# Store and read order at the start of an attention kernel: the first chunk's reads ahead of the second chunk's stores, stores in halves, rows six groups ahead

## The chip, the cores and the metric

One core of one Trainium2 chip runs the whole program. The metric is device time in microseconds (us), the median of several runs. KB are 1024 bytes, as the profile counts them.

## The reference

The reference is an attention layer that mixes its heads before and after the softmax, followed by two dense blocks. The inputs of the attention are 4 batches of 12 heads, 448 rows, 64 columns each.

```python
scores = scale * np.matmul(q, k.transpose(0, 1, 3, 2))
scores = np.einsum('bhij,hg->bgij', scores, w_pre)
scores = scores - np.max(scores, axis=-1, keepdims=True)
attn = np.exp(scores)
attn = attn / (np.sum(attn, axis=-1, keepdims=True) + 1e-09)
attn = np.einsum('bhij,hg->bgij', attn, w_post)
x = np.matmul(attn, v)          # then to 1792 tokens x 768
h = (x @ w1) * (x @ w2) @ w3
x = h @ w_out
h = x @ w_in
out = np.maximum(0.01 * h, h) @ w_out2
```

## The kernel before

The attention comes first, the two dense blocks ("MoE" in the code) after it; this change is all in the first 100 us or so. A batch of 448 rows is cut into four *chunks* of 120, 120, 120 and 88 rows. A chunk is cut into blocks of ten rows, and two blocks make a *group*: a chunk of 120 has six groups, one of 88 has five, the four batches have 92.

One chunk passes through these steps, which the trace shows by tile name and line:

- `qk` (tile `pq`, L203): scores of one pair of heads for all the chunk's rows; ScalarE (and VectorE for the first two chunks) copies them to a tile `s`.
- `flush` (`sdr<-s`, L236): SyncE's queue (SP) stores the scores of two pairs to DRAM. A whole chunk of 120 rows is three stores.
- `relayout` (`sr<-sdr`, L250): SP reads one group's rows back with heads on the partitions, two DMAs a group. It waits for the stores that hold those rows.
- `premix` (`pm`, L261): TensorE mixes the heads of a group.
- softmax on VectorE, ScalarE and GpSimd.
- `postmix` (`po`, L304): TensorE mixes heads again and transposes.
- `av` (`px`, L324): TensorE multiplies with the values `vs`, which `v_prep` (L174) loads once for a batch.

The order is written out by hand. A prologue computes the scores of the first two chunks (`order[0]`, `order[1]`) and starts their stores and reads. Then a loop takes two groups at a time (a *step*): first the stores that have become ready, `qk` of the chunk two ahead, the reads of groups `AHEAD` further on, softmax, `av` of an earlier chunk, `postmix` of the last step's groups, further loads (`side`), and `premix` of the next step's groups. All DMAs of the attention are issued by SP, one after the other; a DMA that waits holds up all behind it. The first `av` stands in the step after the groups 4 and 5 are done, behind `premix` of groups 8 and 9, and `vs` of the first batch is issued in step 2.

The first chunk's stores go in halves of 60 rows already (`HALVES`); groups 0 to 2 need the first half alone.

Of the kernel before, what the change touches and what calls it, by code (L numbers as in the profile page):

```python
# [22 lines left out]
def attention_moe_kernel(ctx: ExitStack, tc, qt, kt, vt, w_pre, w_post, w1, w2, w3t, w_out, w_in2, w_out2, out):  # L23
# [8 lines left out]
    B, _, NPAIR, S = kt.shape  # L32
# [7 lines left out]
    JP = 112  # L40
    NJ = S // JP
    IB = 10
    AHEAD, QAHEAD, HALVES = 4, 2, 2
    HP = 2
    CH = qt.shape[-1]
    scale = 1.0 / float(D) ** 0.5
# [20 lines left out]
    ps = ctx.enter_context(tc.tile_pool(name="ps", bufs=2, space=PSUM))  # L67
    def bank(shape, name):
        return ps.tile(shape, F32, tag="bank", name=name, bufs=8)
# [34 lines left out]
    ends, reads, marks = {}, [], []  # L104

    def attention():
        with ExitStack() as es:
# [47 lines left out]
            kls, qls, stores = {}, {}, []  # L155
# [32 lines left out]
            def qk(b, c, p):  # L188

                m = cols[c]  # L190
                g, r = divmod(p, HP)
                first = (b, c) == order[0]
                if first and p == 0:
                    st[b, c] = late.tile([CH, H, S], F32, tag="ap", name="s", bufs=2)
                elif not first and r == 0:
                    st[b, c] = big.tile([CH, 2 * HP, S], F32, tag="s", name="s", bufs=5)
                t = st[b, c][:, 2 * g * HP:2 * (g + 1) * HP] if first else st[b, c]
                first_two = order.index((b, c)) < QAHEAD
                pq = [bank([CH, S], "pq") for _ in range(2)]
                for j, (x, y) in enumerate(((0, 0), (0, 1), (1, 0))):  # L200
                    for e in range(2):
                        rows = slice(e * D, (e + 1) * D)
                        nc.tensor.matmul(  # L203
                            pq[e][:m], qst[b, c][rows, p, x, :m], kst[b, p][rows, y, :], start=(j == 0), stop=(j == 2)
                        )
                def out():
                    for e in range(2):
                        if e and first_two:
                            nc.vector.tensor_copy(t[:m, 2 * r + e, :], pq[e][:m])
                        else:  # L210
                            nc.scalar.activation(out=t[:m, 2 * r + e, :], in_=pq[e][:m], func=ACTF.Copy)  # L211
                    if r == HP - 1:
                        heads = slice(2 * g * HP, 2 * (g + 1) * HP)
                        if first:
                            n = m // HALVES
                            for i in range(HALVES):
                                stores.append((sdr[b, c][i * n:(i + 1) * n, heads, :], t[i * n:(i + 1) * n]))
                        else:
                            stores.append((sdr[b, c][:, heads, :], t[:m]))

                evs.append(out)
                if first_two:
                    evict()

            evs = []

            def evict():
                while evs:
# [2 lines left out]
            def flush(n=None):  # L231

                while stores and n != 0:
                    n = n and n - 1
                    dst, t = stores.pop(0)
                    nc.sync.dma_start(out=dst, in_=t)  # L236

            def turn(n):

                t = bank([P, P], "turn")  # L240
                for _ in range(n):
                    nc.tensor.matmul(t, ones, ones, start=True, stop=True)  # L242

            def relayout(k):

                sr = srt[k] = wk.tile([P, 2, S], F32, tag="sr", name="sr", bufs=6)
                for s, n in enumerate(groups[k]):
                    b, c, o, nb = blocks[n]
                    src = sdr[b, c][o:o + nb].rearrange("(g i) h j -> (i h) g j", g=2)
                    last = nc.sync.dma_start(out=sr[s * Q:s * Q + nb // 2 * H], in_=src)  # L250
                reads.append(last)
                ends["sync"] = last

            def premix(k):

                sr = srt.pop(k)
                for s, n in enumerate(groups[k]):
                    pms[n] = bank([P, S], "pm")
                    rows = slice(s * Q, s * Q + blocks[n][3] // 2 * H)
                    for g in range(2):  # L260
                        nc.tensor.matmul(  # L261
                            pms[n][g * Q:(g + 1) * Q], kpre[rows], sr[rows, g, :], start=True, stop=True
                        )
# [77 lines left out]
            order = [(b, c) for b in range(B) for c in range(NC)]  # L341
            blocks = [(b, c, o, nb) for b, c in order for o, nb in chunks[c][2]]
            groups, where = [], []
# [5 lines left out]
            NG = len(groups)  # L349
# [15 lines left out]
            for p in range(NPAIR):  # L365
                qk(*order[0], p)
                if p < NPAIR - 1:
                    turn(2 if p < 3 else 1)
                    flush()
                if p == 0:  # L370
                    for low in [k_split(0, 4, nc.gpsimd), k_split(0, 5, nc.gpsimd)]:
                        low()
            q_split(*order[1])()
            constants()
            flush(1)
            for k in range(2):
                relayout(k)
            flush()
            for k in range(2, AHEAD):
                relayout(k)  # L380
            for p in range(NPAIR):
                qk(*order[1], p)
                flush()
            turn(2)
            q_split(*order[2])()

# [2 lines left out]
            def at(step, *job):  # L389

                jobs.setdefault(max(step, 0), []).append(job)
# [14 lines left out]
            for i in range(QAHEAD + 1, len(order)):  # L406
                s0 = firsts[i - QAHEAD] // 2
                at(max(s0 - 2, 2), "qs", *order[i])
                at(s0 - 5, "ql", *order[i])
            for b in range(B):  # L410
                g0 = firsts[b * NC]
                at(g0 // 2 + 2, "v", b)
# [4 lines left out]
                        if p % 2 == 0:  # L417
                            at((g0 + p) // 2 - (4 if b > 1 else 3), "kl", b, p // 2)

            def pairs(k):  # L420

                b, c, t, nt = where[k]
                ci = order.index((b, c))
                if ci + QAHEAD >= len(order):
                    return []
                ps = [4, 5] if nt < NPAIR and t == 4 else [t]
                return [(*order[ci + QAHEAD], p) for p in ps]

            premix(0)
            premix(1)  # L430
            todo = []
            for k in range(0, NG + 2, 2):
                flush()
                while later:
                    stores.append(later.pop(0))
                now = [g for g in (k, k + 1) if g < NG]
                done = [g for g in (k - 2, k - 1) if g >= 0]
                fresh = [n for g in now for n in groups[g]]
                old = [n for g in done for n in groups[g]]
                for g in now:  # L440
                    for x in pairs(g):
                        qk(*x)
                for g in now:
                    if g + AHEAD < NG:
                        relayout(g + AHEAD)
                if fresh:
                    tops(fresh)
                    sm = softmax(fresh)
                evict()
                if now:  # L450
                    for _ in range(min(4 if len(todo) > NPAIR else 2, len(todo))):
                        av(*todo.pop(0))
                    weigh(fresh, sm)
                while lows:
                    lows.pop(0)()
                for i, n in enumerate(old):
                    on_act = i == 1 or i == 3 and k >= firsts[-1 - QAHEAD + 1]
                    postmix(n, nc.scalar.copy if on_act else nc.vector.tensor_copy)
                side(k // 2)
                if k == 4:  # L460
                    while lows:
                        lows.pop(0)()
                for g in done:
                    b, c, t, nt = where[g]
                    if t == nt - 1 and (b, c) != order[-1]:
                        todo += [(b, c, p) for p in range(NPAIR)]
                for g in (k + 2, k + 3):
                    if g < NG:
                        premix(g)
                marks.append(dict(ends))  # L470
# [10 lines left out]
    def moe():  # L481
        with ExitStack() as es:
# [11 lines left out]
            NT = T // P  # L494
            NH = DM // 2
            FQ = 4
            XREADS, XMARKS = (-5, -3), (-5, -5, -4, -4, -4, -4, -3, -3, -3, -2, -2, -2)
            PARTS = ((0, 512), (512, T - 512))

            def behind(mark):  # L500
# [77 lines left out]
            plan = []  # L578
# [91 lines left out]
            for s in range(B // 2):  # L670
                xx = xs[s]
                h = hg.tile([P, KF, 2, T], F32R, tag="hg", name="h")
                for m in range(KF):
# [6 lines left out]
                    for n in range(2):  # L680
                        pb = mm(wb, xx, KM, n)
                        w = PARTS[n][1]
                        at = wk.tile([P, w], F32, tag="at", name="at")
# [10 lines left out]
                for f in range(0, KF2, FQ):  # L694
                    g = hg.tile([P, FQ, 2, T], F32R, tag="hg", name="g")
                    for m in range(FQ):
                        wt = next_w()
                        for n in range(2):
                            pg = mm(wt, x2, KM, n)
                            w = PARTS[n][1]  # L700
                            at = wk.tile([P, w], F32, tag="at", name="gt")
# [25 lines left out]

    attention()
    moe()


# [49 lines left out]
```

## Time and profile before

| | us |
|---|---|
| median of 3 runs (1295.18 to 1295.81) | 1295.79 |
| the profiled execution | 1296.19 |
| its span, first to last instruction | 1294.4 |
| TensorE (PE) busy in the span | 1279.2 |

The profiled execution is 0.40 us above the median, and its time is 1.8 us longer than its span. A stretch of the span is read by its windows (busy time of each engine, granted TensorE clock as a share of full speed, share of time in which the 16 DMA engines are busy, bytes moved), and a wait by what ended it.

### The profile page before, as it was taken

The page shows a single profiled execution, that of the slowest core. Times are in us where ns is not written, and L with a number is a line of the kernel's source. Part 1 is how long each engine was busy: PE and PEld are TensorE (multiplying, and loading weights), DVE is VectorE, ACT ScalarE, POOL GpSimd, SP SyncE. Part 2 cuts the span into 40 slices and gives each one's busy share as a digit, 9 for nine tenths or more (in the row PEclk, how much of TensorE's full clock was granted, in tenths as well). Part 3 has the DMA queues.
Part 4 walks back from the last instruction along what each step waited for, and adds up shares of the span by engine and source line. Part 5 has one row for each costly group of instructions (what it writes and reads, how often), then busy time and mean ns, then how long its engine had stood idle before and what let it go on. Part 6 is the DMA issues. An engine that isn't in the chain of part 4 may idle for free.

```text
span 1294.4 us, 22410 instructions
## 1 busy us (share of the span) xinstructions
PE 1279.2 (99%) x8926; PEld 1127.2 (87%) x8926; DVE 867.4 (67%) x1441; ACT 601.9 (46%) x1169; POOL 117.3 (9%) x192
## 2 busy tenths in 40 slices
PE   7899999999999999999999999999999999999998
PEld 5577777777778989999899999999898889999998
DVE  4565675675668999833485969695673459687662
ACT  5665666676655554522254524352332236434240
POOL 1232232232321000000000000000000000000000
PEclk8899999999999999999999999999999999999999
DMA  7998988988885654733334423363321424342302
GB/s 221 302 319 228 268 261 268 285 266 226 256 261 168 185 163 142 228 115 88 123 105 140 126 95 122 98 218 127 119 82 49 133 77 149 98 147 74 123 1 86
DMA packets 132072, 211.57 MB, mean 163 GB/s; under 512 B 19393, under 2 KB 115649, under 8 KB 131521
## 3 DMA queue, kind: packets, MB, share of 16 engines
q1 hardware_dynamic: 131969, 210.15, 52.6%
q8 instruction: 71, 1.16, 0.4%
q14 instruction: 32, 0.26, 0.1%
HBM read 157.43 MB, written 52.69 MB: 162 GB/s over the span
## 4 chain that ended last, share of the span: by engine, by line
PE 96%; DMA 3%; DVE 1%; ACT 0%; issue 0%; SPq 0%; DVEq 0%
PE pm L619 45%; PE po L716 18%; PE po L304 11%; PE pm L261 6%; PE px L324 6%; PE pw L530 5%; PE pq L203 4%; DMA sr<-sdr 2%; DMA vs<-in_v_dram 1%; PE turn L242 1%; DMA sdr<-s 0%; DVE wc L96 0%; DVE x L75 0%; ACT s L211 0%; DVE ap L311 0%
## 5 line engine op out<-in xcount | busy, mean ns | idle before, releaser
L619 PE MATMUL pm<-x,ws 128*128 128x512 f32 (+1 forms) x2304 | 467.0, 364 | 0.2 <-ACT ws L72 0.2
L619 PEld LDWEIGHTS pm<-x,ws 128*128 128x128 f32 x2304 | 417.6, 188 | 48.0 <-ACT ws L72 0.3
L716 PE MATMUL po<-ws,g 128*128 128x384 f32 x1344 | 234.3, 334 | 0.0
L716 PEld LDWEIGHTS po<-ws,g 128*128 128x128 f32 x1344 | 233.1, 188 | 0.0
L304 PE MATMUL po<-kr,e 128*112 128x120 f32 (+1 forms) x1440 | 159.7, 270 | 0.0
L277 ACT ACTIVATE e<-pm,mx 128x448 f32<-128x448 f32 x180 | 111.8, 632 | 100.0 <-DVE mx L270 99.6
L304 PEld LDWEIGHTS po<-kr,e 128*112 128x112 f32 x1440 | 151.2, 178 | 7.5 <-issue 6.3
L75 DVE TENSOR_TENSOR ws<-wc,ws 128x768 fp32r<-128x768 f32 (+1 forms) x112 | 102.5, 918 | 69.6 <-ACT ws L72 69.0
L72 ACT ACTIVATE ws<-wc 128x768 fp32r<-128x768 f32 (+1 forms) x112 | 90.8, 813 | 113.6 <-PE po L716 73.9
L91 ACT ACTIVATE wc<-wr 128x768 f32<-128x768 f32 (+1 forms) x120 | 104.9, 877 | 78.0 <-DVE ws L75 57.5
L290 POOL TENSOR_SCALAR kr<-kpost,rc 128x120 f32<-128x120 f32 x180 | 113.1, 644 | 276.2 <-DVE rc L287 144.4
L311 DVE COPY ap<-po 112x480 f32<-112x480 f32 (+1 forms) x129 | 83.8, 653 | 55.8 <-PE po L304 55.4
L270 DVE TENSOR_REDUCE mx<-pm 128x1 f32<-128x448 f32 x180 | 101.2, 618 | 25.0 <-PE pm L261 24.6
L619 PE MATMUL pm<-h,ws 128*128 128x512 f32 (+1 forms) x576 | 116.3, 363 | 0.0
L619 PEld LDWEIGHTS pm<-h,ws 128*128 128x128 f32 x576 | 104.3, 188 | 11.7
L99 DVE SCALAR_TENSOR_TENSOR wc<-wr,wc 128x768 uint32<-128x768 uint32 (+1 forms) x120 | 110.3, 920 | 1.6
L96 DVE SCALAR_TENSOR_TENSOR wc<-wr,wc 128x768 uint32<-128x768 uint32 (+1 forms) x120 | 110.0, 919 | 0.9
L261 PE MATMUL pm<-sr,kpre 60*64 60x448 f32 (+1 forms) x720 | 86.0, 567 | 7.0 <-DMA sr<-sdr 6.9
L92 DVE TENSOR_SCALAR wc<-wc 128x768 f32<-128x768 f32 (+1 forms) x120 | 64.8, 540 | 37.9 <-ACT wc L91 37.4
L324 PEld LDWEIGHTS px<-ap,vs 112*64 112x64 f32 x1536 | 73.9, 137 | 17.1 <-ACT e L277 8.2
L723 DVE TENSOR_TENSOR acc<-po,acc 128x384 f32<-128x384 f32 x84 | 46.2, 557 | 62.1 <-PE po L716 61.3
L211 ACT ACTIVATE s<-pq 120x448 f32<-120x448 f32 (+1 forms) x180 | 84.1, 560 | 4.7 <-PE pq L203 4.0
(54 smaller groups left out, 952.8 us busy)
## 6 DMA issues: line engine op xcount, KB each, us to landing
sr<-sdr SPq DMA_DIRECT2D x176, 210.0 KB
wr<-in_moe_w_out_dram SPq DMA_DIRECT2D x40, 768.0 KB
sdr<-s SPq DMA_DIRECT2D x33, 840.0 KB
wr<-in_moe_w_dram SPq DMA_DIRECT2D x32, 768.0 KB
wr<-in_moe_w_in_dram SPq DMA_DIRECT2D x32, 768.0 KB
wr<-in_moe_w_dram SPq DMA_DIRECT2D x16, 512.0 KB
sdr<-s SPq DMA_DIRECT2D x12, 616.0 KB
wf<-w SPq DMA_DIRECT2D x12, 512.0 KB
```

Source lines behind the costliest of these rows:

```text
L75: nc.vector.tensor_tensor(out=dst, in0=src, in1=hi.bitcast(F32), op=ALU.subtract)
L91: nc.scalar.activation(out=cf, in_=hi.bitcast(F32), func=ACTF.Abs)
L96: nc.vector.scalar_tensor_tensor(out=c, in0=hi, scalar=0xC0000000, in1=c, op0=ALU.bitwise_and, op1=ALU.bitwise_or)
L99: nc.vector.scalar_tensor_tensor(out=c, in0=lo, scalar=29, in1=c, op0=ALU.logical_shift_right, op1=ALU.bitwise_or)
L261: nc.tensor.matmul(pms[n][g * Q:(g + 1) * Q], kpre[rows], sr[rows, g, :], start=True, stop=True)
L270: nc.vector.tensor_reduce(out=mxs[n], in_=pms[n], axis=AX.X, op=ALU.max, negate=True)
L277: ends["act"] = nc.scalar.activation(out=ets[n], in_=pms.pop(n), func=ACTF.Exp, bias=mxs.pop(n), scale=1.0, accum_out=sm[:, i:i + 1])
L290: ends["pool"] = nc.gpsimd.tensor_scalar(out=kr[:, i], in0=kpost, scalar1=rc[:, i:i + 1], scalar2=None, op0=ALU.mult)
L304: nc.tensor.matmul(po[:, jc].rearrange("p h (g i) -> p h g i", g=2), e[:, jc * JP:(jc + 1) * JP], kr, start=True, stop=True,)
L324: nc.tensor.matmul(px[e * D:(e + 1) * D, r, :ni], vst[b][:, jc, 2 * p + e, :], ap[:, jc, 2 * p + e, :ni], start=(jc == 0), stop=(jc == NJ ...
L619: nc.tensor.matmul(dst, wt[:, a, kk, :], x[:, kk, c, c0:c0 + w], start=(kk == 0 and j == 0), stop=(kk == kn - 1 and j == 2),)
L716: nc.tensor.matmul(po, g[:, m, a, t * P:(t + 1) * P], wts[m][:, c, 0, cs], start=(m == 0 and j == 0), stop=(m == FQ - 1 and j == 2),)
```

## The change

Nothing is computed otherwise; the same DMAs and matmuls run in another order, and six stores of half the size take the place of three for the second chunk.

- First chunk: of its six half stores, those of the first half of the rows (and one of the second half) go first, then the reads of groups 0 and 1, then the other two halves, then the reads of groups 2 to 5.
- The load of the fourth chunk's q comes next, before the second chunk's stores.
- Second chunk: its stores go in halves too: three first halves and one second half, the reads of groups 6 and 7, and the other two second halves.
- `AHEAD` is 6: groups are read up to six (or eight) ahead, as soon as their chunk's last store was issued one step ago (two, for the further ones).
- The scores of the third chunk are spread over four steps, where they took three.
- The marks behind which the dense block reads its input (`XREADS`) move with the reads.

```diff
-    AHEAD, QAHEAD, HALVES = 4, 2, 2
+    AHEAD, QAHEAD, HALVES = 6, 2, 2
...
+                    if p == NPAIR - 1:
+                        stored[b, c] = step[0]
                     if r == HP - 1:
-                        if first:
+                        if first_two:
                             n = m // HALVES
...
             for p in range(NPAIR):
                 qk(*order[0], p)
                 if p < NPAIR - 1:
                     turn(2 if p < 3 else 1)
+                if p < 3:
                     flush()
...
-            flush(1)
+            late_halves = [stores.pop(i) for i in (1, 2)]
+            flush()
             for k in range(2):
                 relayout(k)
+            stores += late_halves
             flush()
             for k in range(2, AHEAD):
                 relayout(k)
+            q_load(*order[3])
             for p in range(NPAIR):
                 qk(*order[1], p)
-                flush()
+            late_halves = [stores.pop(i) for i in (3, 4)]
+            first_late = stores.pop(1)
+            stores.append(first_late)
+            flush()
...
-                at(s0 - 5, "ql", *order[i])
+                if i > QAHEAD + 1:
+                    at(max(s0 - 5, 2), "ql", *order[i])
...
+            plan = {}
+            for g, (b, c, t, nt) in enumerate(where):
+                ci = order.index((b, c)) + QAHEAD
+                if ci < len(order):
+                    ps = [4, 5] if nt < NPAIR and t == 4 else [t]
+                    for p in ps:
+                        i = (0, 0, 1, 2, 2, 3)[p] if ci == QAHEAD else g // 2
+                        plan.setdefault(i, []).append((*order[ci], p))
...
             premix(0)
             premix(1)
+            for k in range(AHEAD, AHEAD + 2):
+                relayout(k)
+            stores += late_halves
...
-                for g in now:
-                    if g + AHEAD < NG:
-                        relayout(g + AHEAD)
+                for g in range(len(reads), min(k + AHEAD + 2, NG)):
+                    ago = step[0] - stored.get(where[g][:2], step[0])
+                    if ago < (1 if g < k + AHEAD else 2):
+                        break
+                    relayout(g)
...
-            XREADS, XMARKS = (-5, -3), (-5, ...)
+            XREADS, XMARKS = (-3, -1), (-5, ...)
```

SP's queue from the first chunk's stores to the load of `vs`, before. `sdr_0`, `sdr_1`, `sdr_2` are the first three chunks' scores in DRAM; two DMAs `sr<-sdr` make a group.

```order
L236 DMA sdr_0_57<-s 60x1792
L250 DMA sr<-sdr_0_57 60x2x448 x4
L236 DMA sdr_1_58<-s 120x1792 x3
L250 DMA sr<-sdr_0_57 60x2x448 x4
L178 DMA ql<-in_q_dram 128x720
L236 DMA sdr_2_59<-s 120x1792
L250 DMA sr<-sdr_1_58 60x2x448 x4
L178 DMA ql<-in_q_dram 128x720
L236 DMA sdr_2_59<-s 120x1792
L250 DMA sr<-sdr_1_58 60x2x448 x4
L174 DMA vs<-in_v_dram 112x3072
```

Ahead of the first of these rows stand five of the first chunk's half stores and the reads of groups 0 and 1. The same stretch of SP's queue in the changed kernel, from the first chunk's stores on:

```order
L238 DMA sdr_0_57<-s 60x1792 x4
L252 DMA sr<-sdr_0_57 60x2x448 x4
L238 DMA sdr_0_57<-s 60x1792 x2
L252 DMA sr<-sdr_0_57 60x2x448 x8
L178 DMA ql<-in_q_dram 128x720
L238 DMA sdr_1_58<-s 60x1792 x4
L252 DMA sr<-sdr_1_58 60x2x448 x4
L238 DMA sdr_1_58<-s 60x1792 x2
L238 DMA sdr_2_59<-s 120x1792
L252 DMA sr<-sdr_1_58 60x2x448 x8
L178 DMA ql<-in_q_dram 128x720
L174 DMA vs<-in_v_dram 112x3072
```

The reads of groups 4 and 5 moved ahead of the second chunk's stores, and `vs` now stands behind the reads of groups 10 and 11 instead of behind the third chunk's second store.

TensorE's queue from the third pair of premixes (groups 4 and 5) to the first `px`, before:

```order
L261 MATMUL pm<-sr,kpre 64x448 x8
L203 MATMUL pq<-ks,qs 120x448 x12
L304 MATMUL po<-kr,e 112x120 x16
L261 MATMUL pm<-sr,kpre 64x448 x8
L203 MATMUL pq<-ks,qs 88x448 x12
L304 MATMUL po<-kr,e 112x120 x16
L261 MATMUL pm<-sr,kpre 64x448 x8
L203 MATMUL pq<-ks,qs 88x448 x12
L324 MATMUL px<-ap,vs 64x120 x16
```

And in the changed kernel:

```order
L263 MATMUL pm<-sr,kpre 64x448 x8
L203 MATMUL pq<-ks,qs 120x448 x12
L306 MATMUL po<-kr,e 112x120 x16
L263 MATMUL pm<-sr,kpre 64x448 x8
L203 MATMUL pq<-ks,qs 120x448 x6
L203 MATMUL pq<-ks,qs 88x448 x12
L306 MATMUL po<-kr,e 112x120 x16
L263 MATMUL pm<-sr,kpre 64x448 x8
L203 MATMUL pq<-ks,qs 88x448 x12
L326 MATMUL px<-ap,vs 64x120 x16
```

One pair of the third chunk (six matmuls) moved a step later; the first `px` has the same work ahead of it in sum.

## Rows read from the trace of the kernel before

**Rows 1.** The page: span, and busy time of each engine.

```profile
span 1294.4 us, 22410 instructions
PE 1279.2 (99%) x8926; PEld 1127.2 (87%) x8926; DVE 867.4 (67%) x1441; ACT 601.9 (46%) x1169; POOL 117.3 (9%) x192
```

**Rows 2.** Waits of PE over the span: us in total, times, longest.

```profile
PE pm L261 <- DMA sr<-sdr: 6.9, 2, 3.9
```

**Rows 3.** TensorE in order of time, 19 to 66 us: start, length.

```profile
24.31 5.20 PE L261 MATMUL pm<-sr,kpre 60*64 60x448 f32 x16 [3.92 <-DMA sr<-sdr]
...
34.06 1.49 PE L203 MATMUL pq<-ks,qs 64*120 64x448 f32 x12
35.48 3.54 PE L304 MATMUL po<-kr,e 128*112 128x120 f32 x32
42.02 4.15 PE L261 MATMUL pm<-sr,kpre 60*64 60x448 f32 x16 [3.00 <-DMA sr<-sdr]
46.10 2.60 PE L203 MATMUL pq<-ks,qs 64*120 64x448 f32 x12
...
52.73 1.74 PE L261 MATMUL pm<-sr,kpre 60*64 60x448 f32 x16
...
60.91 1.44 PE L203 MATMUL pq<-ks,qs 64*88 64x448 f32 x12
63.86 1.86 PE L324 MATMUL px<-ap,vs 112*64 112x120 f32 x32 [1.51 <-DMA vs<-in_v_dram]
```

**Rows 4.** Long windows: length, then PE, PEld, DVE, ACT, POOL, PEclk, DMA, GB/s.

```profile
18.00:22.00 4.00, 2.38 (x22) 1.76 (x18) 3.51 (x6) 2.81 (x5) 0.00 (x0) 1.00 0.11 33
...
28.00:30.00 2.00, 2.00 (x11) 0.55 (x7) 1.09 (x2) 0.89 (x4) 0.00 (x0) 0.50 0.40 122
...
40.00:42.00 2.00, 0.00 (x0) 0.01 (x1) 0.00 (x0) 0.00 (x0) 0.00 (x0) 1.00 0.87 239
42.00:62.00 20.00, 19.98 (x148) 12.89 (x148) 11.52 (x23) 11.71 (x30) 4.52 (x8) 0.83 1.00 292
...
64.00:390.00 326.00, 326.00 (x3678) 253.48 (x3678) 208.08 (x425) 208.74 (x540) 100.13 (x157) 1.00 0.89 264
```

**Rows 5.** Short windows, the same columns.

```profile
22.00:24.00 2.00, 0.00 (x0) 0.00 (x0) 0.00 (x0) 0.00 (x0) 0.00 (x0) 0.66 0.82 217
...
32.00:34.00 2.00, 2.00 (x18) 0.62 (x16) 0.58 (x2) 0.98 (x2) 1.70 (x4) 0.78 0.92 312
...
42.00:44.00 2.00, 1.99 (x10) 0.75 (x12) 0.62 (x1) 0.26 (x1) 0.00 (x0) 0.78 0.97 309
44.00:46.00 2.00, 2.00 (x9) 0.32 (x4) 1.25 (x2) 1.35 (x5) 0.00 (x0) 0.50 0.95 388
...
48.00:50.00 2.00, 2.00 (x11) 1.44 (x10) 0.07 (x1) 1.56 (x4) 1.76 (x4) 0.51 1.01 250
...
62.00:64.00 2.00, 0.49 (x7) 0.17 (x5) 0.79 (x3) 2.00 (x8) 0.00 (x0) 1.00 0.92 373
```

**Rows 6.** DMA issues over the whole span: count, KB each.

```profile
sr<-sdr SPq DMA_DIRECT2D x176, 210.0 KB
...
sdr<-s SPq DMA_DIRECT2D x33, 840.0 KB
...
ql<-in_q_dram SPq DMA_DIRECT2D x16, 360.0 KB
...
vs<-in_v_dram SPq DMA_DIRECT2D x4, 1344.0 KB
...
sdr<-s SPq DMA_DIRECT2D x6, 420.0 KB
```

**Rows 7.** SP's issues in order of time, 9 to 60 us.

```profile
21.25 1.72 SPq L250 DMA_DIRECT2D sr<-sdr  x4
...
41.18 4.24 SPq L250 DMA_DIRECT2D sr<-sdr  x4
...
51.12 0.33 SPq L174 DMA_DIRECT2D vs<-in_v_dram  x1
```

More of the change, by code (lines that the diff above doesn't have):

```diff
@@ L223, in qk @@
                     evict()
-            evs = []
+            evs, stored, step = [], {}, [-1]
             def evict():
@@ L418, in attention, with pairs @@
                             at((g0 + p) // 2 - (4 if b > 1 else 3), "kl", b, p // 2)
[L420 to L427, printed above, removed]
+            plan = {}
[6 more added lines that the diff above has]
+                        plan.setdefault(i, []).append((*order[ci], p))
+            def pairs(i):
+                return plan.get(i, ())
             premix(0)
             premix(1)
+            for k in range(AHEAD, AHEAD + 2):
+                relayout(k)
+            stores += late_halves
             todo = []
@@ L439, in attention @@
                 old = [n for g in done for n in groups[g]]
-                for g in now:
-                    for x in pairs(g):
-                        qk(*x)
-                for g in now:
-                    if g + AHEAD < NG:
-                        relayout(g + AHEAD)
+                step[0] = k // 2
+                for x in pairs(k // 2):
+                    qk(*x)
+                for g in range(len(reads), min(k + AHEAD + 2, NG)):
[3 more added lines that the diff above has]
+                    relayout(g)
                 if fresh:
@@ L496, in moe @@
             FQ = 4
-            XREADS, XMARKS = (-5, -3), (-5, -5, -4, -4, -4, -4, -3, -3, -3, -2, -2, -2)
+            XREADS, XMARKS = (-3, -1), (-5, -5, -4, -4, -4, -4, -3, -3, -3, -2, -2, -2)
             PARTS = ((0, 512), (512, T - 512))
```

## The prediction

> **What bounds the kernel now.** I read the page first: TensorE is busy 1279.2 us of a span of 1294.4 [rows 1], so at most 15.2 us are idle, and the question is where. The waits of PE answer it: two waits for re-read rows, 6.9 us together [rows 2], and in the order of time also one of 1.51 us for `vs` at the first `px` [rows 3]. From 64 to 390 us PE is busy for 326.00 of 326.00 us at a clock of 1.00 [rows 4]. So all that follows 63.86 us is a chain of matmuls without a hole, and to first order
>
> time = (start of the first `px`) + a fixed rest, plus any slow clock after it.
>
> Work that PE gets done sooner before that point is worth nothing unless the first `px` starts sooner.
>
> Then the windows. The granted clock falls to half behind each of the two long waits: by the shares 0.66 and 0.78 at its ends and 0.50 between, the first stretch lasts from 22.7 to 32.9 us; the second from 43.1 to 50.0 us, 0.9 us of 42 to 44, four whole microseconds and 1.96 of 48 to 50, 6.8 us together [rows 5]. Behind the wait of 1.51 us it stays 1.00 [rows 5].
>
> The DMA engines are the other full resource: share 1.00 at 292 GB/s from 42 to 62 us [rows 4]. What the first `px` waits for, `vs`, is issued at 51.12 [rows 7] and ends PE's wait at 63.86: it queues behind 12 us of transfers. The first 64 us are bound by DMA, the rest by PE.
>
> **The change, part by part.**
>
> *Reads of groups 4 and 5 ahead of the second chunk's stores.* Before, they stand behind three stores of 840 KB [rows 6], 2.58 MB or 8.8 us at 292 GB/s. That takes away the wait of 3.00 us at 42.02. It isn't time gained at the end, only PE's position.
>
> *Fewer stores ahead of the first reads.* One half store of 420 KB moves behind the reads of groups 0 and 1: 0.43 MB, 1.5 us at 292 GB/s, so these reads start near 19.8 instead of 21.25 [rows 7], and the wait of 3.92 us shrinks to 2.4 or less.
>
> *What stands ahead of `vs`.* By the two listings of SP's queue, before: the reads of groups 0 to 9 (20 of 210 KB) and two stores of the third chunk (840 KB each), 5,880 KB. After: the reads of groups 0 to 11 (24) and one such store, 5,880 KB. The stores of the first two chunks, the q and k loads ahead of it are the same bytes. So `vs` can come sooner only by what the DMA engines idled before and idle no more.
>
> That idle time: 18 to 22 us has share 0.11, 3.6 us lost between the last store's data and the first reads; 28 to 30 has 0.40, 1.2 us lost, where the reads of group 3 wait for a store with only two reads (420 KB) queued behind it; 40 to 42 has 0.87, 0.3 us lost, where the reads of group 6 wait until 41.18 [rows 4, 7]. The last is small because a q load and 840 KB stood behind the store that was waited for. After the change, the first gap stays in kind (a store must land before reads); it may shrink, since the last half store has one less ahead, by 0 to 1.3 us (as much as would bring it from 3.6 to 2.3), and I take 0.7. The second stays. The third becomes like the second: the reads of group 6 wait for the second chunk's first halves with one half store, 420 KB, behind them, 1.2 us lost instead of 0.3. Sum for `vs`: -0.7 + 0.9 = +0.2 us. Bounds: -2.0 (first gap down by 1.3, second gone for half, third unchanged) to +1.5 (first unchanged, third gap at 1.8).
>
> *The clock at the first `px`.* PE's work from the first premix to the first `px` is five premix pairs at 1.74, three lots of `pq` at 1.49 and two at 1.44, three `po` at 3.54 [rows 3]: 8.7 + 7.4 + 10.6 = 26.7 us at full clock, in either order. From a first premix at 22.8 it would be done at 49.5 without waits, against 62.35 before, where waits and slow clock cost the difference. In the changed kernel it is held by rows still: between the last rows of group 9 and `vs` stand four reads, a q load and `vs` itself, 840 + 360 + 1344 = 2544 KB [rows 6], 2.6 MB or 8.9 us at 292 GB/s; PE has the last part of a premix (0.4) and one `pq` (1.44) to do meanwhile. So it stands still for about 7 us in one piece ahead of `px`, where it stood for 1.51. Behind `px` is queued all that PE has: `po` of groups 6 and 7, the next premix, and so VectorE's and ScalarE's softmax.
>
> A wait of 3.00 or 3.92 us brought the half clock, one of 1.51 didn't [rows 3, 5]; 7 us is beyond both. What it costs is half the time at half clock while PE has work: in the second stretch 6.8 us, 3.4 us lost; in the first, from PE's return at 24.31 to 32.9, 8.6 us, 4.3 lost. No row shows this stretch after a wait at `px`, so the bounds are 0 (clock doesn't fall) and 4.3. I take 3.4, from the stretch in which PE had work throughout. The Trainium skill (page "TensorE: Matmul & The Clock Gate", section "HAM oscillation — how this bites in real kernels") says the same as a rule, that a wait for DMA longer than the work between waits sends the next work off at half clock, and puts the price at half the throttled time. By it the sum has 3.4 us too, and without it, the waits alone, 0.2 us. The trace agrees: twelve `pq` take 2.60 us in the slow stretch, at 46.10, and 1.49 at full clock, at 34.06 [rows 3].
>
> *The rest, at no cost.* SP issues three DMAs more (the half stores, 0.4 us each on SP); the 8.9 us of transfers queued at that point hide them. Reading groups six ahead, q loads moved, scores spread over four steps: from 64 us on PE never waits for a read as it is, with DMA share at 0.89 [rows 4], so there is nothing to win; and each chunk's first rows come behind the same bytes as before, because they still wait for their own last store. If that cover went, a later read would be late by at most the 840 KB of the two groups read early, 2.9 us, once a chunk.
>
> **Sum.** 1296.19 + 0.2 + 3.4 = 1299.8 for a profiled execution; it lies 0.40 above the median of the runs, so 1299.4 for a median.
>
> **Rivals.**
>
> *The clock costs nothing* (chance 0.27). If slow-clock stretches earlier hold PE back until shortly before `vs` lands, no long idle piece stands ahead of `px`, and the time is that of `vs` alone: 1295.79 + 0.2 = 1296.0, no change. For it: before, two slow stretches did just that, with 1.51 us left. Against: those came with 6.9 us of waits, which shrink now.
>
> *`vs` lands sooner, faster* (0.10). If the gaps in DMA work (3.6 + 1.2 + 0.3 us) closed by more than the clock costs, the first `px` would start at about 61 and PE would run on: 1293. It decides from the point where the saved idle time passes 2.6 us plus the clock's price; the same bytes ahead of `vs` speak against it.
>
> *Reads in lots of eight hurt later* (0.05). Four reads more at once ahead of a store would make one later chunk's rows late by 2.9 us beyond what the read-ahead covers; with its own slow clock (3.4 us) this gives 1299.4 + 6.3 = 1305.7. Against it: 326 us without one wait.
>
> **How the numbers follow.** The forecast has 0.58, the rivals 0.27, 0.10 and 0.05. About 0.2% (2.6 us) is what a measurement here can tell from no change. The forecast's own range is 1297.3 to 1301.5 (clock 1.7 to 4.3, `vs` at -0.2 to +1.4); 0.08 of its 0.58 lies within 2.6 us of before. So slower 0.50 + 0.05 = 0.55, same 0.27 + 0.08 = 0.35, faster 0.10. The range takes in the second case: 1294.8 (`vs` 1 us earlier, no clock lost) to 1301.8 (bounds 1.5 + 4.3, and a little).
>
> **What would show it.** Right: both waits of `pm` for rows shorter, the wait of 3.00 near 42 gone or below 2; the first `px` still starting at 63 to 65 us, after a wait for `vs` of 5 us or more; a granted clock of 0.50 right behind it; no wait of PE from there to 390. Wrong: a first `px` before 62 us (gaps in DMA share near 20, 29 and 40 us closed), or a clock of 1.00 behind a long wait, or a wait for `sr` or `sdr` after 70 us.

## The result and the profile after

The changed kernel takes 1303.28 us, median of 6 runs (1301.56 to 1304.61), against 1295.38 before on the same chip (1294.76 to 1295.81, 6 runs): ratio 1.0061, interval 1.0048 to 1.0074. It is 7.9 us slower; 1299.4 was predicted, at most 1301.8. Its profiled execution took 1303.34 us with a span of 1301.5, against a span of 1294.4 [rows 1].

TensorE's waits after the change (us in total, times, longest), which answer to [rows 2]:

```profile
PE px L326 <- DMA vs<-in_v_dram: 6.1, 1, 6.1
PE pm L263 <- DMA sr<-sdr: 5.1, 5, 2.1
```

TensorE in order of time (start, length), which answers to [rows 3]:

```profile
21.62 1.75 PE L263 MATMUL pm<-sr,kpre 60*64 60x448 f32 x8 [1.19 <-DMA sr<-sdr]
...
36.63 1.73 PE L263 MATMUL pm<-sr,kpre 60*64 60x448 f32 x16
...
55.46 4.14 PE L263 MATMUL pm<-sr,kpre 60*64 60x448 f32 x16 [2.13 <-DMA sr<-sdr]
...
68.14 3.47 PE L326 MATMUL px<-ap,vs 112*64 112x120 f32 x32 [6.06 <-DMA vs<-in_v_dram]
71.53 3.85 PE L306 MATMUL po<-kr,e 128*112 128x120 f32 x32
```

The wait of 3.00 us for the rows of groups 4 and 5 is gone, and PE reaches `premix(4)` at 36.63 instead of 42.02. Then it waits 6.06 us for `vs`, and the first `px` starts at 68.14 instead of 63.86: 4.28 us late. It runs for 3.47 us where it took 1.86, and the `po` behind it for 3.85 where it took 3.53: another 1.9 us. The windows show the clock there, and the gaps in DMA work near 20 and 40 us (columns as in [rows 4, 5]):

```profile
18.00:20.00 2.00, 2.00 (x20) 1.55 (x17) 2.00 (x4) 1.81 (x4) 0.00 (x0) 1.00 0.22 40
20.00:22.00 2.00, 0.81 (x6) 0.46 (x7) 1.55 (x3) 1.05 (x2) 0.00 (x0) 1.00 0.98 262
...
24.00:26.00 2.00, 2.00 (x8) 0.52 (x8) 0.61 (x2) 0.73 (x3) 0.00 (x0) 0.61 0.94 301
...
40.00:42.00 2.00, 2.00 (x22) 2.00 (x21) 0.89 (x3) 2.00 (x7) 0.41 (x1) 1.00 0.47 127
...
58.00:60.00 2.00, 1.99 (x8) 0.59 (x8) 0.99 (x2) 1.43 (x4) 0.00 (x0) 0.64 1.11 258
...
64.00:66.00 2.00, 0.00 (x0) 0.00 (x0) 0.00 (x0) 0.00 (x0) 0.00 (x0) 0.85 1.00 253
66.00:68.00 2.00, 0.00 (x0) 0.00 (x0) 0.00 (x0) 0.00 (x0) 0.00 (x0) 0.50 0.85 351
68.00:70.00 2.00, 1.86 (x20) 1.90 (x22) 0.00 (x0) 0.00 (x0) 0.00 (x0) 0.50 0.96 394
...
72.00:74.00 2.00, 2.00 (x21) 2.00 (x20) 0.71 (x2) 0.22 (x1) 0.00 (x0) 0.95 0.57 237
```

From 72 to 390 us PE is busy for 318.00 of 318.00 us. The two kernels run 6.2 us apart from there; one later step takes 0.4 us more, and where some 0.5 us of the 7.1 us of span go is not known.

SyncE's issues (SPq in the rows) show where `vs` stands now (start, us spent on the group of issues); they answer to [rows 7]:

```profile
18.57 1.87 SPq L252 DMA_DIRECT2D sr<-sdr  x4
...
39.95 3.40 SPq L252 DMA_DIRECT2D sr<-sdr  x4
43.39 2.55 SPq L238 DMA_DIRECT2D sdr<-s  x3
46.04 8.89 SPq L252 DMA_DIRECT2D sr<-sdr  x8
55.39 0.36 SPq L178 DMA_DIRECT2D ql<-in_q_dram  x1
56.20 0.33 SPq L174 DMA_DIRECT2D vs<-in_v_dram  x1
...
59.04 1.22 SPq L238 DMA_DIRECT2D sdr<-s  x2
73.97 1.72 SPq L252 DMA_DIRECT2D sr<-sdr  x4
```

The first reads go out at 18.57 instead of 21.25, but `vs` at 56.20 instead of 51.12. Behind it SyncE stands for 13.1 us, from 60.26 on, until a store of the third chunk has landed; the next `kl` is queued behind that wait.

What the DMA engines moved from 9 us to the first `px`, before (to 63.8) and after (to 68.1): packets, MB, share of the 16 engines:

```profile
DMA packets 4389, 14.15 MB, mean 258 GB/s; under 512 B 526, under 2 KB 2941, under 8 KB 4272
...
q1 hardware_dynamic: 4384, 14.08, 84.0%
```

```profile
DMA packets 4846, 14.18 MB, mean 240 GB/s; under 512 B 617, under 2 KB 3497, under 8 KB 4729
...
q1 hardware_dynamic: 4841, 14.11, 83.7%
```

The same bytes at the same busy share, in 4.3 us more. In time, by these shares, the engines were busy for 46.0 us before and 49.5 after, and idle for 8.8 and 9.6. So 3.4 of the 4.3 us are slower work on the same bytes (306 and 285 GB/s while busy), and 0.9 us are gaps. At 63.8 us the changed kernel was 1.23 MB behind, and half of that it was behind by 45 us. From 9 to 45 us, before and after:

```profile
q1 hardware_dynamic: 2711, 8.64, 76.0%
```

```profile
q1 hardware_dynamic: 2992, 8.03, 76.6%
```

Most of the other half comes from 45 to 55 us. Before:

```profile
DMA packets 1261, 3.10 MB, mean 310 GB/s; under 512 B 141, under 2 KB 959, under 8 KB 1257
...
q1 hardware_dynamic: 1259, 3.08, 98.0%
```

After:

```profile
DMA packets 836, 2.61 MB, mean 261 GB/s; under 512 B 105, under 2 KB 595, under 8 KB 835
...
q1 hardware_dynamic: 835, 2.60, 87.5%
```

What is issued in such a window is not what moves in it. Before, seven reads, two stores, a q load and `vs` were issued in it; after, eight reads and one store. But a read is 120 packets of 1,792 bytes, the ones between 512 bytes and 2 KB, and by them 6.8 reads moved before (818 packets) and 4.1 after (490). Beside these went, after, 240 packets of 7,168 bytes, the 1.72 MB of the second chunk's two late half stores and of a whole one. Two thirds of the missing 0.48 MB are the lower busy share, the rest is 297 GB/s while busy instead of 314. The busy share lies between 0.77 and 0.85 from 48 to 54 us, while SyncE still issues the reads; for eight reads in a row it took 3.80 us in another run (spread scores and early q alone), and 8.89 here.

### The profile page after: what moved, and what is told of

The parts are those of the page before. It is cut to its first block, busy times and chain, and to the rows that moved or that the text cites. A ratio compares the mean times of both kernels' runs of the same rounds, so it can differ in the third digit from the quotient of the medians.

```text
span 1301.5 us, 22413 instructions
## 1 busy us (share of the span) xinstructions
PE 1282.7 (99%) x8926; PEld 1127.5 (87%) x8926; DVE 867.9 (67%) x1441; ACT 601.7 (46%) x1169; POOL 118.4 (9%) x192
## 4 chain that ended last, share of the span: by engine, by line
PE 93%; DMA 4%; DVE 2%; ACT 0%; SPq 0%; issue 0%; POOL 0%; DVEq 0%; POOLq 0%
PE pm L638 45%; PE po L735 18%; PE po L306 10%; PE px L326 5%; PE pm L263 5%; PE pw L549 5%; PE pq L203 5%; DMA sr<-sdr 1%; DMA sdr<-s 1%; DMA vs<-in_v_dram 1%; DMA x<-scr 1%; DVE x L75 1%; DVE mx L272 0%; SPq L252 0%; DMA kl<-in_k_dram 0%; ACT e L279 0%
## 5 line engine op out<-in xcount | busy, mean ns | idle before, releaser
L326 PE MATMUL px<-ap,vs 112*64 112x120 f32 (+1 forms) x1536 | 84.7, 265 | 6.1 <-DMA vs<-in_v_dram 6.1
```

What stands on the lines that cost most here:

```text
L326: nc.tensor.matmul(px[e * D:(e + 1) * D, r, :ni], vst[b][:, jc, 2 * p + e, :], ap[:, jc, 2 * p + e, :ni], start=(jc == 0), stop=(jc == NJ ...
```

## The experiments

Ratios are to the kernel before, on the same chip in the same rounds (medians of before 1295.3 to 1296.9). Starts of the first `px` are of the profiled executions: before 63.86, after 68.14. A single execution of these kernels lies up to some 4 us from its median. Two executions with the same order of transfers up to `vs` (the two runs below that issue it a step sooner in the changed kernel) put `px` at 64.12 and 62.55, so that a difference of 1 or 2 us between two such starts shows little by itself.

**vs one step sooner.** The first explanation was that only the place of `vs` in SyncE's queue had got worse.

```diff
-                at(g0 // 2 + 2, "v", b)
+                at(g0 // 2 + (1 if b == 0 else 2), "v", b)
```

> The changed kernel with the first batch's values (vs) loaded one step earlier, so that the reads of groups 10 and 11 and one q load (1200 KB) stand behind it and no longer ahead. Theory A (the whole time is the start of the first px plus a fixed rest, and that start is set by the bytes ahead of vs): vs lands 1.23 MB at 292 GB/s = 4.2 us earlier, the first px starts near 64 instead of 68.1, time 1297 to 1299. Theory B (a slow stretch of the DMA engines near 44 to 56 us sets it, whatever stands where): the first px starts at 66.5 or later, time 1301.5 or more.

Measured: 1304.64 us, ratio 1.0062 (1.0049 to 1.0075). `px` starts at 64.12, as theory A had it, and nothing is gained. ScalarE later waits for `kl`, and PE for ScalarE:

```profile
84.34 1.04 ACT L72 ACTIVATE ks<-kl 128x448 fp32r<-128x448 f32 x2 [6.14 <-DMA kl<-in_k_dram]
```

So the step "start of the first `px` plus a fixed rest" does not hold in this run: what follows hangs on `kl` too.

**Work for PE ahead of the first px**, so that the clock stays up.

```diff
+                if k == 8:
+                    turn(20)
                 if now:
```

> The changed kernel with 20 dummy matmul calls (128x128, results unused) ahead of the first px, in the wait of 6.06 us for vs. Theory A (half clock behind the wait costs about 2 us: px 3.47 instead of 1.86 us, po 3.85 instead of 3.54): the first px starts at 68 as before but runs in 1.9 us, time 1301.3. Rival (the slow px is due to traffic, or the clock falls anyway): time 1303 or more.

Measured: 1304.62 us, ratio 1.0061 (1.0047 to 1.0075). The first `px` runs at full clock, and the time is lost three steps of the loop later:

```profile
67.91 1.86 PE L326 MATMUL px<-ap,vs 112*64 112x120 f32 x32 [0.77 <-DMA vs<-in_v_dram]
69.70 3.53 PE L306 MATMUL po<-kr,e 128*112 128x120 f32 x32
...
95.67 2.59 PE L326 MATMUL px<-ap,vs 112*64 112x120 f32 x32 [2.48 <-ACT e L279]
```

That ScalarE comes late by a wait of 4.9 us for `kl`. It may be that the 2 us of slow clock in the changed kernel are also 2 us in which transfers catch up; this is not shown, and the profiled execution (1307.54) is the slowest of its five.

**Reads of groups 6 and 7 back in the loop**, behind the other halves.

```diff
-            for k in range(AHEAD, AHEAD + 2):
-                relayout(k)
             stores += late_halves
             todo = []
```

> The changed kernel without the reads of groups 6 and 7 ahead of the loop: they come behind all six half stores of the second chunk and the third chunk's first store. Theory A (SP's wait for the second chunk's first halves, with one half store queued behind it, lets the DMA engines run dry from 39 to 43 us, and vs is late by that): DMA share near 1 through that stretch, the first px at 66 or earlier, time 1301 or less. Rival (half stores themselves, or something at 44 to 56 us, make it late): first px at 67.5 or later, time 1302.5 or more.

Measured: 1303.66 us, ratio 1.0053 (1.0041 to 1.0066). No gain: twelve reads now stand in a row and take SyncE 13.98 us, `vs` goes out at 56.85, and `px` starts at 69.06. The gap in DMA work at 40 us is filled (share 0.96 from 40 to 42 us), and another has opened from 46 to 50 (0.61 and 0.45).

**The first chunk's part alone**, on the kernel before.

```diff
+                if p < 3:
                     flush()
...
-            flush(1)
+            late_halves = [stores.pop(i) for i in (1, 2)]
+            flush()
             for k in range(2):
                 relayout(k)
+            stores += late_halves
             flush()
-            for k in range(2, AHEAD):
+            for k in range(2, AHEAD + 2):
...
-                    if g + AHEAD < NG:
+                    if len(reads) <= g + AHEAD < NG:
```

> The kernel before with the first chunk's part alone: two of its half stores behind the reads of groups 0 and 1, and the reads of groups 2 to 5 ahead of the second chunk's stores, which stay whole; groups four ahead, all else as before. Theory A (the loss comes from the second chunk's halves and their waits; the first chunk's part moves only waits): first px at 63 to 65, time 1294.5 to 1298. Rival (bringing the first chunk's reads forward is itself the loss): first px at 67 or later, time 1301 or more.

Measured: 1295.89 us, ratio 0.9991 (0.9983 to 1.0000). This part costs nothing. It wins 0.96 us at `px`, and ScalarE's wait for `kl` takes back 0.86:

```profile
62.90 1.86 PE L324 MATMUL px<-ap,vs 112*64 112x120 f32 x32 [1.94 <-DMA vs<-in_v_dram]
```

The loss therefore lies in the other three parts. Each was undone in the changed kernel, or added by itself to this one.

**Second chunk's stores whole again.**

```diff
-                        if first_two:
+                        if first:
                             n = m // HALVES
...
-            late_halves = [stores.pop(i) for i in (3, 4)]
-            first_late = stores.pop(1)
-            stores.append(first_late)
             flush()
...
-            stores += late_halves
```

> The changed kernel with the second chunk's stores whole again and none of them kept back; the loop's rules, the early q and the reads stay as changed. The kernel with the first chunk's order alone ran at 1295.9, the changed one at 1303.3: 7.4 us lie in the rest. Theory H (the second chunk's halves put too few bytes under way behind small reads, the DMA share of 0.65 between 38 and 44 us): the share there is over 0.9, vs is issued at 52 or 53 us, and the time is 1295 to 1298. Theory S (the third chunk's stores come late because its scores are spread over four steps) and theory R (reads eight at a time and far ahead) : nothing of it changes, 1301 to 1304, with SP's wait of some 13 us ahead of group 12's reads still there.

Measured: 1303.54 us, ratio 1.0055 (1.0042 to 1.0068). Without the halves the loss stays, so theory H falls as the one cause; `px` starts at 68.20. Nor is the DMA share from 38 to 44 us over 0.9, as theory H had it: it is 0.62.

**Third chunk's scores over three steps again.**

```diff
-                        i = (0, 0, 1, 2, 2, 3)[p] if ci == QAHEAD else g // 2
+                        i = g // 2
```

> The changed kernel with the third chunk's scores over three steps of the loop, as before, so that its second and third stores are issued a step sooner; all else as changed. Theory S: SP's wait of 13.1 us ahead of group 12's reads falls to about the 7.1 us of before, the first px starts 4 to 6 us sooner and the time is 1296 to 1299. Theory H: 1301 to 1304, with the DMA share of 0.65 between 38 and 44 us unchanged. Theory R: 1301 to 1304.

Measured: 1307.43 us, ratio 1.0087 (1.0074 to 1.0100), slower still. Theory S falls. In this run the third chunk's second store (840 KB) is ahead of `vs` again, beside the same reads, and `px` starts at

```profile
69.36 3.47 PE L326 MATMUL px<-ap,vs 112*64 112x120 f32 x32 [11.22 <-DMA vs<-in_v_dram]
```

1.22 us later than in the changed kernel. As a price of that store this is weak: it is within what two starts can differ by, the profiled execution is 1.8 us quicker than its median, and by the ratios this run is 3.4 us above the changed kernel.

**Reads four groups ahead again.**

```diff
-                for g in range(len(reads), min(k + AHEAD + 2, NG)):
-                    ago = step[0] - stored.get(where[g][:2], step[0])
-                    if ago < (1 if g < k + AHEAD else 2):
-                        break
-                    relayout(g)
+                for g in now:
+                    if len(reads) <= g + 4 < NG:
+                        relayout(g + 4)
...
```

> The changed kernel with the loop's reads by the rule of before (four groups ahead, four reads a step), so from group 8 on the reads stand where they stood before; halves, spread scores and early q as changed. Theory R: the reads of groups 8 to 11 no longer stand in a lot of eight ahead of kl, and the time is 1296 to 1299. Theories H and S: 1301 to 1304.

Measured: 1300.81 us, ratio 1.0044 (1.0030 to 1.0058), the one undoing that helps clearly, short of the 1296 to 1299 expected. The reads of groups 10 and 11 go behind `vs`, and `px` starts 3.32 us sooner, still at half clock:

```profile
64.82 3.47 PE L326 MATMUL px<-ap,vs 112*64 112x120 f32 x32 [3.99 <-DMA vs<-in_v_dram]
```

**Second chunk's halves alone**: the changed kernel with the last two edits and with the fourth chunk's q load where it was, so the first-chunk kernel plus the halves and their reads.

> The kernel before with the first chunk's order and the second chunk's halves and reads as changed, but with scores over three steps, reads four groups ahead and q where it was. It differs from the kernel that ran at 1295.9 by the second chunk's halves and their order alone. Theory H: 1301 to 1304. Theories S and R: 1295 to 1297.

Measured: 1299.73 us, ratio 1.0031 (1.0019 to 1.0043): by the ratios some 5 us above the first-chunk kernel. That is between the ranges, nearer to theory H's 1301: something is lost here, though the halves' removal above gave nothing clear back. `px` starts at 65.08, 2.18 us later than there, and at half clock. But the halves are not the only thing that differs: a q load now stands behind them, ScalarE waits 5.5 us for it and TensorE 4.08 us behind that, at 49.83, and the store and `vs` come later in SyncE's queue. In the changed kernel, which loads this q early, that wait is not there. So what the halves cost there this run does not show.

**Six groups ahead alone**: the first-chunk kernel with only the changed rule for reads.

> The kernel with the first chunk's order alone and of the changed loop only the rule of reading six groups ahead. The four reads of groups 10 and 11 (840 KB) stand ahead of vs, which they did not there. Theory O: the first px starts 2.5 to 4 us later than 62.90, its columns run at half the clock (1.6 us more), and the time is 1299 to 1302. Theory B: the bytes are moved sooner and not more often, so what vs loses groups 10 and 11 win; 1295.5 to 1298.

Measured: 1301.64 us, ratio 1.0046 (1.0033 to 1.0058), in the range of theory O. In the profile `px` starts 1.99 us later than in the first-chunk kernel, a little under the 2.5 expected, at half clock:

```profile
64.89 3.47 PE L326 MATMUL px<-ap,vs 112*64 112x120 f32 x32 [4.93 <-DMA vs<-in_v_dram]
68.29 4.71 PE L306 MATMUL po<-kr,e 128*112 128x120 f32 x32
```

What the DMA engines moved from 9 us to the first `px`, in the first-chunk kernel (to 62.9) and in this one (to 64.9):

```profile
q1 hardware_dynamic: 4428, 14.15, 84.8%
```

```profile
q1 hardware_dynamic: 4932, 15.00, 87.5%
```

The 0.85 MB more took 3.2 us more of busy time, at 310 and 307 GB/s while busy, and 1.2 us of gaps were filled. Here the reads cost about what their bytes say.

**Spread scores and early q alone** on the first-chunk kernel: the second chunk's stores whole, reads four groups ahead.

> The kernel with the first chunk's order alone, and of the changed loop only the third chunk's scores over four steps and the early q; the second chunk's stores whole, reads four groups ahead. In SyncE's order the third chunk's second store (840 KB, 2.9 us at 290 GB/s) now stands behind vs. Theory O: vs lands no later than 63, but groups 10 and 11, read behind that chunk's later stores, are late at their premix or kl is; 1294.5 to 1298. Theory B: 1295 to 1297, no wait over 2 us. If the spread alone is the cause of the loss, 1300 to 1303.

Measured: 1297.68 us, ratio 1.0015 (1.0006 to 1.0024), as theory O had it, with `kl` late. The first `px` waits for nothing, at 63.16; 1.75 us are lost two steps of the loop later, where ScalarE waits 4.1 us for `kl`.

**vs and kl both a step sooner**, on the changed kernel and on the first-chunk kernel.

```diff
-                at(g0 // 2 + 2, "v", b)
+                at(g0 // 2 + (1 if b == 0 else 2), "v", b)
...
-                            at((g0 + p) // 2 - (4 if b > 1 else 3), "kl", b, p // 2)
+                            at((g0 + p) // 2 - 4, "kl", b, p // 2)
```

> The changed kernel with two loads issued one step of the loop sooner: vs of the first batch, and the kl of the second batch. Before this only vs was moved, and the 4 us that it won at the first px were lost again at the wait for kl. Theory O (what counts is what stands ahead of vs and then of kl in SyncE's order): with both moved the first px starts at 62 to 65 us, ACT no longer waits over 2 us for kl, and the time is 1295 to 1298. Theory B (the DMA engines have fallen behind as a whole by some 1 MB, 3 to 4 us at 290 GB/s, and some transfer always pays): the wait turns up at another tile, the rows sr of groups 10 to 13 or q, and the time stays at 1300 to 1305.

> The kernel with the first chunk's order alone (1295.9, first px at 62.90 after a wait of 1.94 for vs, ACT waiting 2.48 for kl at 70.36) with vs and the second batch's kl one step sooner. Theory O: px starts at 61 to 62, the later px is no longer held by kl, and the time is 1293.5 to 1295. Theory B: 1295.5 to 1298, with rows of sr waited for in place of vs.

Measured: 1302.72 us, ratio 1.0047 (1.0033 to 1.0062), and 1298.16, ratio 1.0018 (1.0009 to 1.0028). Theory B held both times (the second lies 0.2 us above its range): in the first `px` starts at 62.55, and PE waits 1.86 us at 82.77 for rows; in the second PE waits 1.72 us at 60.16 for rows, and `px` starts at 66.69. The first profiled execution, 1306.31, is the slowest of its six. In both, what came sooner at one place was lost at another.

**The load of vs taken away**, with and without the change.

```diff
+            vst[0] = late.tile([JP, NJ, H, D], F32, tag="vs", name="vs", bufs=2)
+            nc.gpsimd.memset(vst[0], 1.0)
...
-                at(g0 // 2 + 2, "v", b)
+                if b:
+                    at(g0 // 2 + 2, "v", b)
```

> The changed kernel without the load of vs for the first batch: that tile is filled with ones on GpSimd early on, so the first batch's output is not the reference's and 1,344 KB (4 to 5 us of the DMA engines) are not moved. Theory B (bytes: the DMA engines are behind as a whole): the first px starts when PE comes to it, near 62.1, and nothing is lost again at kl or the rows; 1295 to 1297. Theory O (SyncE's order: its 13 us wait for a store holds up kl and the rows behind it, whatever the engines carry): px at 62, but some 4 us come back at kl or at the rows of groups 12 and 13; 1299 to 1303.

> The kernel before without the first batch's load of vs, in the same way. It is the measure for the kernel above. px waits 1.51 for vs there, so either theory gives 1293.5 to 1295 if nothing else holds PE; if the DMA engines are the bound of this stretch before the change too, its later waits at kl go as well.

Measured: 1298.55 us, ratio 1.0017 (1.0004 to 1.0030), and 1294.11, ratio 0.9985 (0.9976 to 0.9994). With 1.38 MB less to move the distance between the two kernels shrinks from 7.9 to 4.4 us, but does not vanish: the time lies between theory B's 1297 and theory O's 1299. The profile, of one of its quickest executions (1295.98), shows part of the rest. `px` starts at 59.00, 4.86 us ahead of before; then SyncE stands at a store, the DMA engines run dry, and `kl` goes out behind it. Windows, SyncE and ScalarE of that kernel:

```profile
66.00:68.00 2.00, 2.00 (x26) 1.46 (x28) 1.49 (x3) 2.00 (x7) 0.00 (x0) 1.00 0.15 53
```

```profile
67.03 2.44 SPq L252 DMA_DIRECT2D sr<-sdr  x4
69.52 0.39 SPq L178 DMA_DIRECT2D ql<-in_q_dram  x1
70.01 0.38 SPq L162 DMA_DIRECT2D kl<-in_k_dram  x1
```

```profile
76.36 1.04 ACT L72 ACTIVATE ks<-kl 128x448 fp32r<-128x448 f32 x2 [4.76 <-DMA kl<-in_k_dram]
```

A DMA share of 0.15 while SyncE waits is, for these 2 us, no debt of bytes; it is the queue's order. That step of the loop takes 4.0 us longer than before.

**kl alone a step sooner**, on the first-chunk kernel and on the one with spread scores.

> The kernel with the first chunk's order alone, with the second batch's kl one step sooner and vs where it was. That kernel won 0.97 us at the first px and lost 0.86 where ACT waited 2.48 for kl. If only the place of kl does this: 1294.0 to 1295.3. If kl ahead of the rows makes the rows or vs late: 1296 to 1299.

> The kernel with the first chunk's order, the spread scores and the early q (1297.7; first px at 63.16 without a wait, then 1.75 lost where ACT waited 4.1 for kl at step 7), with kl one step sooner. If only the place of kl does this: 1294.3 to 1296.3. If the DMA engines owe as much in any order: 1297 to 1300.

Measured: 1296.47 us, ratio 1.0003 (0.9994 to 1.0012), and 1296.02, ratio 1.0000 (0.9992 to 1.0009). The second came out as the place of `kl` alone would have it, by the ratios 1.9 us below the same kernel with `kl` late. The first fell in the other range, but not shown for the reason given there: the longest wait for rows, 3.6 us, ends at 47.14, before `kl` is issued at 50.99. No version that does the whole work was clearly faster than the kernel before.

## Why the prediction was wrong

**Right: the direction, and why.** PE's own progress before `vs` was worth nothing. The wait of 3.00 us went, the one of 3.92 became 1.19 (2.4 or less was forecast), and PE then stood still for 6.06 us (about 7 was forecast) ahead of `px`, with the clock at 0.50 behind it and no wait from there to 390 us. The gap foreseen where the reads of group 6 wait is there: DMA share 0.47 from 40 to 42 us, where it was 0.87 [rows 4].

**Failed: "`vs` moves only by what the DMA engines idle", +0.2 us.** It moved by 4.28. The bytes were counted rightly, 14.08 and 14.11 MB. What failed is the step from bytes to time: all transfers were put at one rate, 292 GB/s, whatever their order, so that a new order of the same bytes cost nothing. In the changed kernel the same bytes took 49.5 us of busy time instead of 46.0, at 285 GB/s instead of 306, and these 3.4 us are most of the 4.28. The sum had no term for them.

The idle time grew by 0.9 us, inside the bounds, but this was in part luck. The first gap, from 18 to 22 us, fell from 3.6 to 1.6 us, by 2.0 where 0.7 was taken and 1.3 was the bound. The third, from 38 to 44 us, grew from 0.5 to 2.1 us, by 1.6 where 0.9 was forecast. And a gap that no term had opened from 44 to 54 us, 1.3 us, where there was 0.1 before (before and after):

```profile
44.00:54.00 10.00, 10.00 (x69) 6.57 (x64) 4.71 (x9) 5.70 (x14) 2.26 (x4) 0.70 0.99 325
```

```profile
44.00:54.00 10.00, 8.20 (x64) 5.41 (x62) 5.24 (x10) 5.86 (x15) 2.26 (x4) 1.00 0.87 243
```

Why the rate fell is not shown. That reads are dearer than a store, 840 KB against 840 KB, would be one reason, and the starts of `px` seem to say so: 3.32 us for the four reads taken out of the changed kernel, 1.99 added to the first-chunk kernel, 1.22 for the store. But these are single executions, two of which can differ by 1.6 us with the same order, and with six groups ahead alone the rate stayed at 307 GB/s. The second chunk's halves alone are not the reason either: with them whole again, all else changed, the same reckoning gives 288 (14.13 MB, 83.0%, to 68.2 us).

The Trainium skill (page "DMA: Bandwidth & Descriptors", section "Specifications") gives 512 bytes as the least transfer for line rate. By it the reads, in pieces of 448 float32 values or 1,792 bytes, should cost as much per byte as the stores, in pieces of 7,168. By the packet records in the trace of the kernel before, the two took 54 and 52 ns per KB from 9 to 390 us, which agrees, and 58 and 47 from 9 us to the first `px`, which agrees less well.

**Failed too: "a fixed rest".** The experiments on `vs` and `kl` show two ends of one stretch: in these runs the DMA engines and SyncE's queue set the pace beyond the first `px`, to the wait for ScalarE that ends at 95.67 in one of them, and PE's holes are only where this shows. The rival "reads in lots of eight hurt later" named a late wait for rows; what came late was `kl`, behind SyncE's wait for a store. It lasts 13.1 us; before, SyncE's issues show 7.1 at that place, from 59.33 to 66.47:

```profile
59.04 0.29 SPq L236 DMA_DIRECT2D sdr<-s  x1
66.47 1.97 SPq L250 DMA_DIRECT2D sr<-sdr  x4
```

**Mis-sized: the clock.** Forecast 3.4 us, measured 1.93 (3.47 for 1.86 and 3.85 for 3.53). The 3.4 came from a stretch in which PE worked throughout; here the clock had fallen by 66 us, and 2 us of its low stretch passed with PE idle. The Trainium skill's rule (page "TensorE: Matmul & The Clock Gate", section "HAM oscillation — how this bites in real kernels") agrees as to the wait at `px`: the clock fell in it. Its price, half the throttled time, agrees with the 1.93 us only if the time in which PE had no work is left out. Elsewhere in this trace the clock fell behind shorter waits: to 0.61 from 24 to 26 us, behind waits of 1.19 and 0.64 us, both under the 1.51 that I had read as too short, and to 0.64 from 58 to 60, behind one of 2.13 us. And the price is not final: with the clock kept up, 1304.62 us.

**Failed: "the rest, at no cost".** Adding the parts one to another gives ratios of 0.9991 (first chunk), 1.0015 (with spread scores and early q), 1.0044 (with the second chunk's halves) and 1.0061 (with six groups ahead): -1.2, +3.1, +3.8 and +2.2 us; each ratio is known to some 1 to 2 us. In another order they have other sizes: halves alone +5, six ahead alone +7 above the first-chunk kernel, and the spread scores, +3.1 with the early q on that kernel, save 3.4 where the halves and the six groups ahead are in (1.0061 with them, 1.0087 without). I had read the cover from the stretch behind 64 us, at DMA share 0.89, while these edits act ahead of it, where the share was 1.00 [rows 4].

**Open.** How the loss divides between bytes and order isn't settled by one number: without `vs` 3.5 of 7.9 us go and 4.4 stay, one of whose causes is seen (SyncE's wait ahead of `kl`). Why the same bytes moved more slowly in the new order was not tried by itself.

## What to carry to other kernels

Where the DMA engines are full, a new order of transfers is judged by what stands ahead of each load that somebody waits for, and equal bytes do not make equal time: here the same 14.1 MB went at 306 GB/s of busy time in one order and at 285 in another. One mean rate over a mixed stretch hid that such a difference was possible. What a window of the profile moved is read from its packets by size, not from the DMAs issued in it. A wait removed upstream is a gain only if the next load on the same queue also comes sooner, so follow the queue past the first consumer, to the one after it. A read put far ahead in a queue that is issued in order makes everything behind it wait for the store that it reads: here `kl`, for 13.1 us.

## What was not expected of the hardware

The DMA engines' share of busy time does not tell how many bytes they move: up to the first `px` it was 84% in both kernels, at 258 and at 240 GB/s over the stretch. By the packet records of the two traces it was the single packets that took longer: those of 1,792 bytes 109 ns in the mean where they took 101, those of 7,168 bytes 356 where they took 329, their median 272 in both. Of the latter, those that started from 46 to 54 us, when the two late half stores and a whole store moved, took 413 ns in the mean after the change, and 280 before it.
